# Three wide blocks in place of four, a longer hold for attention matmuls, and a margin in the planner that orders a fused attention and MLP kernel

## The chip, the cores and the metric

One core of a Trainium2 chip runs the whole program. The metric is device time in microseconds, from the start to the end of one execution; a kernel's time is the median of its runs. Engines: PE is TensorE (its weight loads, PEld, overlap its matmuls), DVE is VectorE, ACT is ScalarE, POOL is GpSimd, SP is SyncE, which here issues all DMAs.

## The reference

Linear attention with exponential features (batch B = 8, H = 8 heads, S = 576 tokens, head size D = 64, 128 features and their negatives), then a two-layer MLP on the 4608 tokens with 512 and 2048 columns, all in float32:

```python
def phi(x):
    proj = einsum('bhsd,df->bhsf', x, w_phi)
    proj = proj - max(abs(proj), axis=-1, keepdims=True)
    return concatenate([exp(proj), exp(-proj)], axis=-1)
q_p, k_p = phi(q), phi(k)
kv  = einsum('bhsf,bhsd->bhfd', k_p, v)
z   = sum(k_p, axis=2)
num = einsum('bhsf,bhfd->bhsd', q_p, kv)
den = einsum('bhsf,bhf->bhs', q_p, z)[..., None] + 1e-06
x   = (num / den).transpose(0, 2, 1, 3).reshape(4608, 512)
h   = x @ w_in                       # 512 -> 2048
g   = 0.5 * h * (1 + erf(h / sqrt(2)))
out = g @ w_out                      # 2048 -> 512
```

## The kernel before

**Precision.** An MLP operand is split into a high and a low part in the format fp32r, and a product is three matmuls (high by high, high by low, low by high). Attention matmuls are plain float32 on small shapes, except the later query projections.

**Attention, per batch element** (`attention`). Four heads form a quad (`k_quad`), two a pair (`q_pair`). A quad has five units; each projects keys into the PSUM tile `pk`, DVE takes the maximum (`mx`) and subtracts it (`ek`), ACT makes two exponentials, and small matmuls add into `kv`, which ACT copies to `kvn`. A pair has two halves of 288 tokens: DVE splits the query (`qh`), PE projects it into `pq`, ACT copies it to `pc`, POOL takes a maximum over partitions (`mb`), DVE subtracts, ACT makes exponentials (`ef`), PE multiplies them with `kvn` into `pn`, ACT copies `xo`, and SP writes it to DRAM (`x_d`). The denominators go through DVE and POOL (`un`, `db`) to DRAM, and `quotients` loads them (`dc`), inverts them on DVE and writes `r_d`. From the third batch element on, `pk` and `pq` share one PSUM buffer, the tag `pp`: ten key units and eight query halves use it in turn for each element.

**MLP, narrow** (`block`): 256 tokens, eight units of two of the sixteen column groups. A unit has 24 first-layer matmuls of 256 columns into `ph` (two buffers), two Gelu passes on ACT (`gh`, and `ph` in place), a subtraction on DVE (`gl`), and 12 second-layer matmuls of 512 columns into `po`.

**MLP, wide** (`wide_block`): 512 tokens. The first layer uses seven products in place of eight (Strassen's scheme as Winograd wrote it), on sums of weight blocks that `combos` makes once and stores in DRAM (`s_d`), and on sums of inputs. A unit has 42 first-layer matmuls of 256 columns into `pa` and `pb`, DVE additions that put the outputs together (`u`, `c`), Gelus, and 24 second-layer matmuls into two banks (`po_po`, `po_pp`). Its inputs and the sums `s` lie in buffers that attention used before, so `combos` and the wide blocks are gated on the last 60 operations of attention (`GATE`).

**Order.** Every operation is entered into a planner (`Plan.op`) with an engine, an estimated cost and a rank. `Plan.order` simulates the engines with these costs and picks, at each step, the operation that can start first, and among those that can start within 0.02 us the one with the lowest rank. `emit` then issues everything in that order. On the chip each engine runs its own queue in program order and waits on semaphores; the planner's times are not waited for. PE operations of attention get `PULL` = -2000 on their rank, so they go before MLP matmuls, unless `hold` applies: after an MLP matmul, attention operations wait until those that are ready cost `LUMP` together, or one of them has waited `LINGER`. `plan.since` keeps operations back until a planned time (`WPACE` for each weight, `TF` for the MLP, `HOLD2` for the third and later batch elements). `T0`, `T15`, `LEAD`, `WR`, `ATR`, `WSPAN` set ranks. The ten narrow blocks come first (`2 * JW`), then the four wide ones.

Of the kernel before, what the change touches and what calls it, by code (L numbers as in the profile page):

```python
# [25 lines left out]
DM, DFF = 512, 2048  # L26
# [3 lines left out]
TB = 256  # L30
NBLK = NT // TB
NCC = DM // P
# [27 lines left out]
class Plan:  # L60
# [57 lines left out]
    def order(self, bias):  # L118
# [13 lines left out]
        n = len(self.ops)  # L132
# [40 lines left out]
        while len(done) < n:  # L173
            best = None
            for e, lst in cand.items():
                if not lst:
                    continue
                opts = []
                for o in lst:
                    t = start_of(o)  # L180
                    if t is not None:
                        opts.append((t, o))
                if not opts:
                    continue
                t0 = min(t for t, _ in opts)
                lim = max(t0, clock[e]) + 0.02
                hold = 0.0
                if e == "pe" and last[0] == "f":
                    t_of = {id(o): max(o.ready, first.setdefault(o.n, t)) for t, o in opts}
                    there = [o for t, o in opts if t <= lim and o.kind != "f"]  # L190
                    if sum(o.cost for o in there) < LUMP and all(lim - t_of[id(o)] < LINGER for o in there):
                        hold = 4000.0
                key = None
                for t, o in opts:
                    if t <= lim:
                        k = o.rank
                        if e == "act" and o.table is not None and o.table != table[0]:
                            k += bias
                        if o.kind != "f":
                            k += hold  # L200
                        if key is None or (k, o.n) < key[0]:
                            key = ((k, o.n), t, o)
                if best is None or key[1] < best[1]:
                    best = key
            if best is None:
                raise RuntimeError("no operation can go")
            _, t, o = best
            cand[o.eng].remove(o)
            cost = o.cost
            if o.eng == "act" and o.table is not None and o.table != table[0]:  # L210
                cost += self.SWITCH
                table[0] = o.table
            if o.eng == "pe":
                if self.SHAPE[last[0]] != self.SHAPE[o.kind]:
                    cost += self.BEHIND[last[0]] + self.BEFORE[o.kind]
                last[0] = o.kind
            if o.eng == "dve" and not o.psum:
                for span in taken[-4:]:
                    if t < span[1] - 0.3 and t + cost > span[0] + 0.3 and not span[2]:
                        span[2] = True  # L220
                        cost += BLOCKED
            if o.eng == "pool":
                taken.append([t, t + cost, False])
            o.start, o.end = t, run(t, cost, o.duty) if o.eng == "pe" else t + cost
            if o.nbytes:
                dge[0] = max(dge[0], t) + 0.55
                dma[0] = max(dma[0], dge[0] + 0.75) + o.nbytes / 350.0
                o.late = dma[0] + 0.15 - o.end
            if o.table == "gelu":
                gelus[0] += 1  # L230
                left_at[0] = o.end
            clock[o.eng] = o.end
            for b in o.bufs:
                if b.tag is not None and not b.held:
                    f = slot_free_at[b.tag]
                    b.slot = turn[b.tag]
                    f[b.slot] = None
                    turn[b.tag] = (b.slot + 1) % len(f)
                    b.held = True
                    assert b.line.pop(0) is b  # L240
                b.left -= 1
                if b.left == 0 and b.tag is not None:
                    slot_free_at[b.tag][b.slot] = o.end + o.late + self.HOP[o.eng]
            for u in o.users:
                u.wait -= 1
                u.ready = max(u.ready, o.end + o.late + (self.HOP if u.eng != o.eng else self.SAME)[o.eng])
                if u.wait == 0:
                    cand[u.eng].append(u)
            done.append(o)
# [10 lines left out]
def mm_cost(m, n):  # L260
    return max(0.875 * m, n / 2.306 + 9) / 1e3
# [27 lines left out]
def fused_kernel(ctx: ExitStack, tc: tile.TileContext, qT, kT, va, w_st, w_in, w_out, out):  # L289
# [15 lines left out]
    op = plan.op  # L305
# [60 lines left out]
    wi, wo = {}, {}  # L366
# [223 lines left out]
    NU = NFC // 2  # L590

    def block(j, rank):
# [3 lines left out]
        xh = sb["xh"]([P, NCC, TB], F32R, f"xh_{j}")  # L596
        xl = sb["xl"]([P, NCC, TB], F32R, f"xl_{j}")
        t = j * TB
# [19 lines left out]
        for u in range(NU):  # L618
            rk = rank(u / NU)
            ph = ps["ph"]([P, 2, TB], F32, f"ph_{j}_{u}")  # L620
            for i in range(2):

                def mm1(ph=ph, u=u, i=i):
                    ins = []
                    f = 2 * u + i
                    fs = slice(f % 4 * P, f % 4 * P + P)
                    for c in range(NCC):
                        for w, x in ((0, xh), (0, xl), (1, xh)):
                            ins.append(mm(ph()[:, i, :], lhsT=wi[c, f // 4]()[:, w, fs], rhs=x()[:, c, :], start=len(ins) == 0, stop=len(ins) == 11))
                    return ins  # L630

                op("pe", 12 * mm_cost(128, TB), mm1, r=[xh, xl] + [wi[c, u // 2] for c in range(NCC)], w=[ph], rank=rk)
            gh = sb["gh"]([P, 2, TB], F32R, f"gh_{j}_{u}")
            gl = sb["gl"]([P, 2, TB], F32R, f"gl_{j}_{u}")
            op("act", act(2 * TB, True) + 0.016, lambda gh=gh, ph=ph: nc.scalar.activation(gh(), ph(), AF.Gelu), r=[ph], w=[gh], table="gelu", rank=URGE + rk)  # L635
            op("act", act(2 * TB, True) + 0.037, lambda ph=ph: nc.scalar.activation(ph(), ph(), AF.Gelu), r=[ph], w=[ph], table="gelu", rank=URGE + rk)  # L636
            tt("dve", dve(2 * TB, True), gl, ph, lambda gh=gh: gh().bitcast(F32), ALU.subtract, [ph, gh], [gl], rank=URGE + rk, psum=True)
            for i in range(2):

                def mm2(u=u, i=i, gh=gh, gl=gl):  # L640
                    ins = []
                    f = 2 * u + i
                    for m in range(2):
                        ms = slice(m * P, (m + 1) * P)
                        for g, w in ((gh, 0), (gh, 1), (gl, 0)):
                            ins.append(mm(po()[:, m], lhsT=g()[:, i, ms], rhs=wo[f]()[:, w, :], start=f == 0 and len(ins) % 3 == 0,
                                                        stop=f == NFC - 1 and len(ins) % 3 == 2))
                    return ins

                op("pe", 6 * mm_cost(128, DM), mm2, r=[gh, gl, wo[2 * u + i]], w=[po], rank=rk)  # L650
# [37 lines left out]
    def wide_block(j, rank):  # L688
# [4 lines left out]
        for hh in range(2):  # L693
            x = raw[hh]
# [49 lines left out]
        for u in range(NU):  # L744
# [13 lines left out]
            def product(n, bank, z, first, sides=sides):  # L758
                a, r = sides[n]

                def go():
                    ins = []
                    for i in range(2):
                        for w, x in ((0, 0), (0, 1), (1, 0)):
                            ins.append(mm(bank()[:, z], lhsT=a(i, w), rhs=bs[n]()[:, x, i], start=first and not ins, stop=len(ins) == 5,
                                          skip_group_check=True))
                    return ins

                op("pe", 6 * mm_cost(128, TB), go, r=[*r, bs[n]], w=[bank], rank=rk)

            uu = sb["kvn"]([P, TB], F32, f"u2_{j}_{u}")
            u3 = sb["xo"]([P, TB], F32, f"u3_{j}_{u}")
# [14 lines left out]
            product(4, Bk, 1, False)  # L787
            add(a1, uu, b0, [uu, Bk], [A])
            add(lambda C=C: C()[:, 0], uu, b1, [uu, Bk], [C])
            for f, at, psum in ((f1, A, True), (f2, C, False)):  # L790
                gh = sb["gh"]([P, 2, TB], F32R, f"gh_{j}_{f}")
                gl = sb["gl"]([P, 2, TB], F32R, f"gl_{j}_{f}")
# [3 lines left out]
                for t in range(2):  # L796
# [7 lines left out]
                                              stop=u == NU - 1 and f != f1 and len(ins) % 3 == 2))  # L804
                        return ins

                    op("pe", 6 * mm_cost(128, DM), mm2, r=[gh, gl, wo[f]], w=[po[t]], rank=rk)
        for t in range(2):
            for m in range(2):
                ob = sb["ob"]([P, DM], F32, f"ob_{j}_{t}_{m}")  # L810
# [39 lines left out]


SB = 2
JW = 5
CR = 100.0
CSPAN = 100.0
GATE = 60
T15 = 937.149
BIAS = 40
STICK = 2
PATIENCE = 2.661  # L860
URGE = -1000.0
EARLY = 37.497
WPACE = 2.294
WSPAN = 5.119
WARM = 4
EARLY_PK = ("pp", "po")
EARLY_E = ("ek", "xh", "ek", "xl")
BLOCKED = 0.9
HOLD2 = 26.359
EB = 2  # L870
KB = 0
EPACE = 20.0
TF = 77.984
ND = 2
LUMP = 0.626
LINGER = 0.643
PAIR_K = 0.43
PAIR_Q = 0.7
PAIR_N = 1.18
PAIR_V = 0.125  # L880
PULL = -2000.0
LEAD = 290.175
HOLD = 39.176
WR = -5.223
ATR = -4.775
T0 = 47.571
VERBOSE = False


# [36 lines left out]
```

## Time and profile before

| | before |
|---|---|
| median of 3 runs | 1167.02 us (1164.23 to 1170.59) |
| profiled execution, its own time | 1165.43 us |
| its span, first to last instruction | 1163.7 us |
| mean granted TensorE clock | 0.989 |
| PE busy | 1094.6 us, 94% of the span |
| DVE, ACT, POOL busy | 719.0, 592.9, 327.9 us |

The time lies 1.7 us above the span. A busy PE is not a PE at its peak: matmuls are pipelined, and each record lasts longer than the distance to the next one. The granted clock is the share of full speed that PE was given.

### The profile page before, as it was taken

The numbers are of one execution on the slowest core, as the hardware profiler recorded it, in microseconds if no ns is written. First come the engines' busy times: TensorE is split into PE (matmuls) and PEld (weight loads), VectorE is DVE, ScalarE is ACT, GpSimd is POOL, SyncE is SP. The second block draws the span as 40 slices with busy tenths as digits, with TensorE's granted clock in tenths as the row PEclk, the third lists the DMA queues.
The fourth block names the chain that finished last, engine by engine and source line by source line (L and its number), as shares of the span: only waits on it lengthen the run. The fifth ranks groups of instructions, "written<-read, shape, count | busy, mean of one in ns | idle before, by whom it ended". The sixth has DMA issues, their size and how long they took to land.

```text
span 1163.7 us, 22198 instructions
## 1 busy us (share of the span) xinstructions
PE 1094.6 (94%) x8904; PEld 909.2 (78%) x8904; DVE 719.0 (62%) x1209; ACT 592.9 (51%) x1001; POOL 327.9 (28%) x116
## 2 busy tenths in 40 slices
PE   7888989999999999999989999999999999899997
PEld 4546767877777778877868878889898899798995
DVE  6998999387777676776675644555534534524331
ACT  6876786657676666766757651121222322322322
POOL 2331224166665556765544440000000000000000
PEclk9999999999999999999989999999999999999999
DMA  9974412224233242252131115443724634623420
GB/s 335 338 253 131 111 50 67 82 81 119 68 110 90 79 117 83 64 149 62 53 88 42 53 38 127 145 128 98 209 84 124 184 92 125 185 89 117 128 73 37
DMA packets 117175, 133.98 MB, mean 115 GB/s; under 512 B 28288, under 2 KB 87840, under 8 KB 117072
## 3 DMA queue, kind: packets, MB, share of 16 engines
q1 hardware_dynamic: 117072, 132.56, 38.5%
q8 instruction: 70, 1.15, 0.4%
q14 instruction: 33, 0.27, 0.1%
HBM read 104.96 MB, written 27.56 MB: 114 GB/s over the span
## 4 chain that ended last, share of the span: by engine, by line
PE 59%; DVE 17%; DMA 10%; ACT 4%; issue 4%; SPq 2%; POOL 2%; POOLq 0%; DVEq 0%; ACTq 0%
PE po L308 12%; PE ph L308 9%; PE pb L308 7%; PE po_po L308 7%; PE po_pp L308 7%; PE pa L308 5%; PE kv L308 4%; PE pn L308 3%; DMA qt<-in_qT_dram 3%; PE pq L308 2%; PE pk L308 2%; DVE gl L334 2%; POOL db L548 2%; DVE qh L334 2%; DMA dc<-d_d 1%
## 5 line engine op out<-in xcount | busy, mean ns | idle before, releaser
L308 PE MATMUL ph<-xh,w_i 128*128 128x256 f32 x1280 | 249.0, 285 | 1.8 <-DVE gl L334 1.8
L548 POOL PARTITION_ALL_REDUCE db<-un x48 | 178.4, 3716 | 160.1 <-DVE un L545 120.3
L308 PEld LDWEIGHTS ph<-xh,w_i 128*128 128x128 f32 x1280 | 204.7, 189 | 10.4 <-issue 2.6
L308 PE MATMUL po<-w_o,gh 128*128 128x512 f32 x640 | 207.6, 406 | 2.9 <-ACT ob L328 1.7
L513 POOL PARTITION_ALL_REDUCE mb<-pc x64 | 152.0, 2375 | 205.1 <-ACT pc L328 182.8
L308 PE MATMUL ph<-xl,w_i 128*128 128x256 f32 x640 | 181.4, 283 | 0.0
L308 PE MATMUL po<-w_o,gl 128*128 128x512 f32 x320 | 129.4, 404 | 11.5 <-DVE gl L334 11.5
L308 PEld LDWEIGHTS po<-w_o,gh 128*128 128x128 f32 x640 | 116.4, 192 | 30.1 <-issue 2.4
L793 ACT ACTIVATE gh<-pa 128x512 fp32r<-128x512 f32 x32 | 19.2, 599 | 217.7 <-DVE pa L334 215.3
L308 PEld LDWEIGHTS ph<-xl,w_i 128*128 128x128 f32 x640 | 120.9, 189 | 1.7
L308 PEld LDWEIGHTS kv<-vt,ek 128*64 128x64 f32 (+1 forms) x2560 | 83.5, 137 | 36.6 <-ACT ek L447 17.9
L308 PE MATMUL kv<-vt,ek 128*64 128x65 f32 (+1 forms) x2560 | 94.9, 225 | 10.2 <-ACT ek L447 8.9
L635 ACT ACTIVATE gh<-ph 128x512 fp32r<-128x512 f32 x80 | 47.9, 598 | 108.7 <-PE ph L308 100.6
L308 PE MATMUL pn<-ef,kvn 128*64 128x288 f32 (+1 forms) x512 | 97.0, 422 | 3.3 <-ACT xo L328 1.7
L519 ACT ACTIVATE ef<-pc 128x576 f32<-128x576 f32 x128 | 81.7, 679 | 33.6 <-DVE pc L334 33.3
L334 DVE TENSOR_TENSOR pa<-u,pb 128x256 f32<-128x256 f32 x32 | 13.7, 428 | 130.8 <-PE pb L308 130.8
L447 ACT ACTIVATE ek<-ek 128x512 f32<-128x512 f32 (+1 forms) x120 | 69.4, 586 | 47.1 <-DVE ek L334 45.6
L334 DVE TENSOR_TENSOR gl<-ph,gh 128x512 fp32r<-128x512 f32 x80 | 54.9, 687 | 50.0 <-ACT ph L636 47.2
L308 PEld LDWEIGHTS po<-w_o,gl 128*128 128x128 f32 x320 | 61.1, 191 | 31.2 <-DVE gl L334 17.5
L430 DVE TENSOR_REDUCE mx<-pk 128x4 f32<-128x512 f32 (+1 forms) x80 | 50.5, 631 | 53.5 <-PE pk L308 53.3
L308 PE MATMUL po_po<-w_o,gh 128*128 128x512 f32 x256 | 80.0, 394 | 1.1 <-ACT gh L793 1.1
L308 PE MATMUL pb<-b,s 128*128 128x256 f32 x576 | 79.1, 282 | 2.0 <-DMA s<-s_d 1.9
(90 smaller groups left out, 1905.2 us busy)
## 6 DMA issues: line engine op xcount, KB each, us to landing
s<-s_d SPq DMA_DIRECT2D x128, 256.0 KB
qt<-in_qT_dram SPq DMA_DIRECT2D x112, 144.0 KB
vt<-in_va_dram SPq DMA_DIRECT2D x16, 585.0 KB
kt<-in_kT_dram SPq DMA_DIRECT2D x16, 576.0 KB
out_dram<-ob SPq DMA_DIRECT2D x36, 256.0 KB
raw_i<-in_w_in_dram SPq DMA_DIRECT2D x16, 512.0 KB
raw_o<-in_w_out_dram SPq DMA_DIRECT2D x16, 512.0 KB
x_d<-xo SPq DMA_DIRECT2D x48, 144.0 KB
```

What stands on the lines that cost most here:

```text
L308: return tc.keep_in_program_order(nc.tensor.matmul(*a, **kw))
L334: op(eng, cost, lambda: e.tensor_tensor(out=dst(), in0=a(), in1=b(), op=o), r=r, w=w, **kw)
L430: op("dve", dve(256 * n, True), lambda xs=xs, mx=mx: nc.vector.tensor_reduce(out=mx()[:, 0].rearrange("p (j i) -> p j i", j=2), in_=xs(), ...
L447: op("act", act(256 * n, b < SB), lambda at=at, es=es, s=s: nc.scalar.activation(es[s](), at(), AF.Exp, scale=1.0 - 2.0 * s), r=[of], w=[e ...
L513: op("pool", 2.2, lambda mb=mb, pc=pc: nc.gpsimd.partition_all_reduce(mb(), pc(), P, bass_isa.ReduceOp.absmax), r=[pc], w=[mb], **k(1))
L519: op("act", act(2 * HS), lambda ef=ef, pc=pc, s=s: nc.scalar.activation(ef()[:, s], pc(), AF.Exp, scale=1.0 - 2.0 * s), r=[pc], w=[ef], ta ...
L548: op("pool", 3.7, lambda db=db, un=un: nc.gpsimd.partition_all_reduce(db(), un(), P, bass_isa.ReduceOp.add), r=[un], w=[db], **k())
L635: op("act", act(2 * TB, True) + 0.016, lambda gh=gh, ph=ph: nc.scalar.activation(gh(), ph(), AF.Gelu), r=[ph], w=[gh], table="gelu", rank= ...
L793: op("act", act(2 * TB, psum) + 0.016, lambda gh=gh, at=at: nc.scalar.activation(gh(), at(), AF.Gelu), r=[at], w=[gh], table="gelu", rank= ...
```

## The change

`JW` goes from 5 to 6: twelve narrow blocks and three wide ones in place of ten and four. `LUMP` and `LINGER` go from 0.626 and 0.643 us to 2.5 and 3.0 us. In the planner, an operation of PE that uses the result of another engine counts as ready 0.8 us later (`MARGIN`), from planned time 130 on; a buffer that comes free is not delayed so. First-layer matmuls get the rank of a point 1.5 units earlier (`AHEAD`, `AHEADW`). In the last unit of a wide block the second layer is entered by output bank first, in the others by column group first as before. The constants of rank and pace are replaced.

```diff
-                u.ready = max(u.ready, o.end + o.late + (self.HOP if u.eng != o.eng else self.SAME)[o.eng])
+                u.ready = max(u.ready, o.end + o.late + (self.HOP if u.eng != o.eng else self.SAME)[o.eng] + (MARGIN if u.eng == "pe" != o.eng and o.end > 130.0 else 0.0))
...
-                op("pe", 12 * mm_cost(128, TB), mm1, r=[xh, xl] + [wi[c, u // 2] for c in range(NCC)], w=[ph], rank=rk)
+                op("pe", 12 * mm_cost(128, TB), mm1, r=[xh, xl] + [wi[c, u // 2] for c in range(NCC)], w=[ph], rank=rank((u - AHEAD) / NU))
...
-                op("pe", 6 * mm_cost(128, TB), go, r=[*r, bs[n]], w=[bank], rank=rk)
+                op("pe", 6 * mm_cost(128, TB), go, r=[*r, bs[n]], w=[bank], rank=rank((u - AHEADW) / NU))
...
+            second = []
...
-                    op("pe", 6 * mm_cost(128, DM), mm2, r=[gh, gl, wo[f]], w=[po[t]], rank=rk)
+                    second.append((t, f != f1, mm2, [gh, gl, wo[f]]))
+            for t, _, go, r in sorted(second, key=lambda x: x[:2] if u == NU - 1 else (x[1], x[0])):
+                op("pe", 6 * mm_cost(128, DM), go, r=r, w=[po[t]], rank=rk)
...
-JW = 5
+JW = 6
+AHEAD = 1.5
+AHEADW = 1.5
+MARGIN = 0.8
...
-T15 = 937.149
+T15 = 901.4
...
-PATIENCE = 2.661
+PATIENCE = 2.5
...
-EARLY = 37.497
-WPACE = 2.294
-WSPAN = 5.119
+EARLY = 37.5
+WPACE = 3.996
+WSPAN = 24.5
...
-HOLD2 = 26.359
+HOLD2 = 0.0
...
-TF = 77.984
+TF = 90.0
...
-LUMP = 0.626
-LINGER = 0.643
+LUMP = 2.5
+LINGER = 3.0
...
-LEAD = 290.175
-HOLD = 39.176
-WR = -5.223
-ATR = -4.775
-T0 = 47.571
+LEAD = 167.4
+HOLD = 44.6
+WR = -13.5
+ATR = -21.1
+T0 = 57.4
```

## Rows read from the trace of the kernel before

**Rows 1.** Busy time by stretch (stretch, length, PE PEld DVE ACT POOL, PEclk, DMA, GB/s)
```profile
90.00:180.00 90.00, 79.73 (x677) 62.01 (x678) 84.27 (x140) 70.75 (x120) 21.59 (x8) 0.96 0.33 88
180.00:693.00 513.00, 490.07 (x4556) 399.59 (x4555) 354.21 (x530) 342.19 (x518) 278.32 (x93) 0.99 0.29 82
693.00:808.00 115.00, 110.21 (x703) 98.48 (x702) 62.37 (x121) 24.20 (x45) 0.28 (x1) 1.00 0.43 120
808.00:1164.00 356.00, 341.05 (x2111) 303.46 (x2110) 142.88 (x296) 91.15 (x178) 0.00 (x0) 1.00 0.41 120
```

**Rows 2.** Chain that ended last, 780 to 860 us (start, us, what)
```profile
792.33 5.71 PE ph L308 x48
798.04 5.54 PE po L308 x24
```

**Rows 3.** PE busy time by stretch, matmuls of tile ph alone
```profile
90.00:693.00 603.00, 193.35 (x1463) 0.98 0.29 83
693.00:808.00 115.00, 55.66 (x460) 1.00 0.43 120
```

**Rows 4.** The same for kv, pk, pn and pq, in this order
```profile
90.00:693.00 603.00, 72.18 (x1984) 0.98 0.29 83
...
90.00:693.00 603.00, 40.75 (x432) 0.98 0.29 83
...
90.00:693.00 603.00, 69.73 (x424) 0.98 0.29 83
...
90.00:693.00 603.00, 40.72 (x208) 0.98 0.29 83
```

**Rows 5.** What PE waited for, 90 to 693 us (total, times, longest)
```profile
PE pq L308 <- DVE ek L334: 9.7, 8, 4.3
PE po L308 <- DVE gl L334: 8.4, 7, 2.2
```

**Rows 6.** What PE waited for, 693 to 1164 us
```profile
PE po_po L308 <- DVE gl L334: 5.0, 7, 1.5
PE po L308 <- DVE gl L334: 3.1, 4, 1.3
```

**Rows 7.** Timeline of PE, end of the span
```profile
1157.54 0.40 PE L308 MATMUL po_pp<-w_o,gl 128*128 128x512 f32 x1
```

**Rows 8.** Timeline of ACT, end of the span
```profile
1156.58 1.07 ACT L328 COPY ob<-po_po 128x512 f32<-128x512 f32 x2 [3.58 <-PE po_po L308]
1159.29 1.21 ACT L328 COPY ob<-po_pp 128x512 f32<-128x512 f32 x2 [1.63 <-DMA out_dram<-ob]
```

**Rows 9.** Timeline of PE, 240 to 280 us (start, us)
```profile
240.79 1.19 PE L308 MATMUL pn<-ef,kvn 128*64 128x288 f32 x8
241.91 0.71 PE L308 MATMUL pk<-wst,kt 64*128 64x128 f32 x8
...
248.74 0.28 PE L308 MATMUL ph<-xh,w_i 128*128 128x256 f32 x1
248.94 1.19 PE L308 MATMUL pn<-ef,kvn 128*64 128x288 f32 x8
...
250.29 0.28 PE L308 MATMUL ph<-xl,w_i 128*128 128x256 f32 x1
```

**Rows 10.** Granted clock in a short stretch (stretch, length, PE busy, PEclk, DMA, GB/s)
```profile
605.00:609.00 4.00, 4.00 (x12) 0.55 0.02 2
```

**Rows 11.** Timelines of PE, DVE and POOL, around 528 and 600 us
```profile
603.50 1.30 PE L308 MATMUL pq<-qh,wd 128*128 128x288 f32 x4 [4.33 <-DVE ek L334]
...
528.80 2.64 DVE L334 TENSOR_TENSOR qh<-qt,qh 64x576 fp32r<-64x576 f32 x1
...
597.18 1.03 DVE L568 TENSOR_SCALAR dc<-dc 128x18 f32<-128x18 f32 x1 [3.93 <-DMA dc<-d_d]
...
528.03 3.85 POOL L548 PARTITION_ALL_REDUCE db<-un  x1
```

**Rows 12.** Instructions on tile qh, DVE (count: min/median/max ns, first and last start)
```profile
L334 DVE TENSOR_TENSOR qh<-qt,qh x48: 754/756/2968, 133.4 to 670.7; 64x576 fp32r<-64x576 f32 x48
```

## Prediction

> **What bounds the kernel now.** I read the busy time by stretch first. From 693 us on only MLP work is left (POOL, which serves attention, has 0.28 us there), and PE is busy for 110.2 of 115 us and then 341.05 of 356 [rows 1]. Before that, from 90 to 693 us, attention and narrow blocks share PE: 79.73 + 490.07 = 569.8 us busy of 603, 33.2 idle [rows 1]. PE is the engine that sets the end; DVE is close behind only from 90 to 180 (84.27 of 90), while the weights are split, and falls to 354.21 of 513 after that [rows 1].
>
> Busy time hides how fast PE really goes, so the second view is the chain that ended last: 48 first-layer matmuls pass in 5.71 us, 0.119 us each, and 24 second-layer ones in 5.54 us, 0.231 each [rows 2]. A narrow block has 192 and 96 of them: 22.8 + 22.2 = 45.0 us. In 90 to 693, 1463 first-layer matmuls ran [rows 3], 7.6 blocks, hence 343 us; attention's own PE time is 72.18 + 40.75 + 69.73 + 40.72 = 223.4 us [rows 4]. With the idle 33.2 that is 600 of the 603 us, so the account closes. What can be won without less work is that idle, the holes inside attention's visits, and about 5 us on either side of 808 us.
>
> The third view is who PE waits for. Nearly all of it comes from DVE: query projections for the shared bank that DVE has yet to read (9.7 us in 8 waits, the longest 4.3) and second-layer matmuls for `gl` (8.4 in 7) [rows 5], and after 693 again `gl`, 5.0 + 3.1 in 11 [rows 6]. The queue of PE is written out by the planner, so an operation placed before its input is there stops everything behind it, first-layer matmuls included that were ready.
>
> **The change part by part.** The sum goes against the profiled execution's own 1165.4 us; the median of the runs shown is 1.6 us above it, and I add that at the end.
>
> *One wide block becomes two narrow ones.* A wide block has 8 units of 42 first-layer matmuls, 336; two narrow ones have 384. The second layer is the same, 192. So PE gets 48 x 0.119 = **+5.7 us** of work at full rate, and nothing hides it, since PE sets the end. The planner only orders; it can't take that back.
>
> *Block boundaries.* In 693 to 808, 460 first-layer matmuls ran [rows 3], 2.4 narrow blocks with 4.8 us idle: 2.0 each. In 808 to 1164 the idle is 15.0 us [rows 1], of which 6 lie behind the last matmul near 1158 [rows 7]: 9 over four wide blocks, 2.2 each. Swapping one for two gives 4.0 - 2.2 = **+1.8**.
>
> *The last unit of a wide block by bank.* `po_po` is now complete two groups of six second-layer matmuls (2 x 1.39) before the end in place of one. At the end of the span ACT copies `po_po` at 1156.58, then waits for the output DMA to free the two `ob` buffers, and copies `po_pp` at 1159.29 [rows 8], though its last matmul ended at 1157.9 [rows 7]. With `po_po` copied 1.4 us earlier, this wait of 1.63 us nearly goes: **-1.3**. In exchange the second column group's Gelus have only one group of six matmuls to hide behind; if they don't, the next late thing is `gl` of that group, at most 1.4 us back. Bounds: 0 to -1.6.
>
> *Margin and first layer ahead.* Second-layer matmuls are now placed as if `gl` came 0.8 us later, and first-layer matmuls of the next unit go ahead of them. The chip doesn't wait for planned times, so the margin costs nothing by itself; the work that fills is 12 first-layer matmuls, 1.43 us, already waiting with a free `ph`. The waits concerned add up to 8.4 + 5.0 + 3.1 = 16.5 us in 18, 0.9 each [rows 5, 6]. Below: all vanish, 16.5. Above: nothing, if DVE is late by more than the order allows. I take half, **-8**, since the longest waits (2.2, 1.5, 1.3) exceed the margin. If the cover is gone (no free `ph`), the first layer itself waits for `gl`, and nothing is won.
>
> *Holding attention.* An attention operation that comes after an MLP matmul is now held until 2.5 us of company are ready or 3.0 us have passed. This covers what the margin doesn't: the bank that comes free. Of the 9.7 us of `pq` waits the longest is 4.3 [rows 5]; a hold of up to 3.0 leaves little of the others. Below: the 9.7 and a part of the 15 us of small waits that the two rows don't list (33.2 - 18.1), say 17; above: nothing. I take **-8**. Behind a held projection stand DVE's `mx` and `ek`, ACT's exponentials and `kv`; they are late by the same, which matters only if attention runs out of time (a rival below).
>
> *Visits to PE.* Between first-layer matmuls a `pn` group takes from 248.74 + 0.12 to 250.29 - 0.12, 1.31 us; followed by `pk` it takes 1.12 (240.79 to 241.91) [rows 9]. So a visit costs about 0.19 us beyond its work. The shared bank is used 18 times per batch element, 108 times for six, so I estimate some 110 visits now. Of 223.4 us in portions of at least 2.5 there are at most 89: 20 fewer; at 54, half, it would be 10 us. I take 20 x 0.19 = **-4**, bounds 0 and -10. The Trainium skill (TensorEngine Tiling (Array Packing), Key Properties) says that a change of tiling mode drains TensorE, which would hold between `pn` and `pk` as well. By that, merging two visits saves one change of four and not half of the price, so -2 and a sum 2 us higher; the rows show no more for `pn` before `pk` than 1.12 us.
>
> *Clock.* After long waits the granted clock falls to the lower of its two levels, 1.2 GHz, for a while: 0.55 of full speed on average in 605 to 609 [rows 10], behind the wait of 4.33 us that ended at 603.50 [rows 11]. By the stretches, 0.04 x 90 + 0.01 x 513 = 8.7 us of PE's rate are lost [rows 1]. With the longest waits shortened I take **-3**, bounds 0 and -8.7.
>
> *Slower weights, MLP from planned 90 in place of 78.* DVE splits the weights at 84.27 of 90 us busy [rows 1], so later loads hide behind DVE, and attention gets DVE's time instead: I take 0. If the cover fails, the MLP starts 12 us later (the difference of `TF`), of which attention fills a part. Bounds: -5 (earlier loads of queries) to +12.
>
> Sum: 1165.4 + 5.7 + 1.8 - 1.3 - 8 - 8 - 4 - 3 = 1148.6, and with 1.6 for the median **1150 us**, 1.4% less than before.
>
> **The rivals.**
>
> *The order moves the waits but doesn't remove them.* DVE is late by more than any margin here: the subtraction of `qh` takes 0.756 us as a rule and up to 2.968 [rows 12]; at 528.80 it took 2.64 beside POOL's all-reduce of 3.85 us [rows 11]. And DVE stands in its own queue: 3.93 us for the denominators' DMA until 597.18, just ahead of PE's wait of 4.33 [rows 11]. A margin of 0.8 doesn't hold 1.9 or 3.9. Then margin, hold and clock give nothing: 1165.4 + 5.7 + 1.8 - 1.3 - 4 = 1167.6, 1169 for the median. Against it: most waits are short (0.9 on average), and the hold is longer. The Trainium skill (SBUF — State Buffer, Terms, the shared port pair) calls this an exclusive lock, in which the later of the two engines is blocked for the whole instruction. By that rule a DVE operation can be late by all of an all-reduce, which points to this rival; the 2.64 us agree.
>
> *Attention comes too late.* Today 108 uses of the shared bank take 603 us, 5.6 each. The hold grows by up to 2.4 us (3.0 - 0.643). Twelve narrow blocks, attention and today's idle give 540 + 223 + 33 = 796 us of PE; so attention outlasts them once a use takes 796 / 108 = 7.4 us, 1.8 more than now. At 2.4 more, narrow work ends near 862 (573 us of it and 0.258 of the time for attention), with 11 uses left; unheld, they take 62 us, in which PE has 24 us of work, and the wide blocks still need their sums, gated on attention: some 20 us of DVE (62.37 busy in 693 to 808 [rows 1], a third of it). About 58 us idle: near 1208, slower. Against it: during a visit nothing is held, so one visit can serve two uses, and the planner falls back to attention where PE has nothing else.
>
> *The start loses its cover.* The 12 us of `TF` appear and half of the gains fails: 1150 + 12 + 11 = 1173.
>
> **Chances and range.** The forecast's mechanism 0.57 (own range 1130 to 1161); waits only moved 0.19 (1163 to 1172); start 0.12 (1161 to 1180); attention late 0.12 (1180 to 1225). A measurement of this kernel can tell about 0.5%, 1161.2 to 1172.9, from no change. Faster: 0.57. Same: 0.15 of the second, 0.05 of the third, 0.20 together. Slower: 0.04 + 0.07 + 0.12 = 0.23. All bounds below at once give 1165.4 + 7.5 - 1.6 - 16.5 - 17 - 10 - 8.7 - 5 + 1.6 = 1116; I set the low end at 1124 and the high end at 1186, where the early part of the late case begins.
>
> **What would show it.** First-layer matmuls 2304 in narrow tiles and 1008 in wide ones; `po` waits for `gl` below 8 us in the mixed stretch; `pq` waits for DVE below 4; fewer, longer visits; no stretch with a clock near 0.6; attention over before the twelfth narrow block. Wrong would be: PE idle between the last `pn` and the first `pa`, a first `ph` 12 us later than before, or the waits back under other names.

## The result, and the profile after

The median fell from 1165.62 us (4 runs, 1161.07 to 1170.59) to 1148.99 us (4 runs, 1147.43 to 1151.56): a ratio of 0.9867, 95% interval 0.9837 to 0.9898. The forecast was 1150. The profiled execution spans 1145.7 us, 18.0 less than before.

The page of the changed kernel: engine, busy time, share and instructions; the granted clock in 40 slices.

```profile
PE 1097.1 (96%) x8952; PEld 920.4 (80%) x8952; DVE 696.2 (61%) x1153; ACT 662.2 (58%) x1045; POOL 321.5 (28%) x116
...
PEclk9998987999999999999999999999999999999999
```

PE has 48 more matmuls than before and is busy 2.5 us longer, in a span 18.0 us shorter. The clock digits below 9 all lie in the first seven slices, the first 200 us.

Busy time of PE by stretch, first of the kernel before and then of the changed one (stretch, length, busy, granted clock, DMA share, GB/s):

```profile
90.00:210.00 120.00, 107.72 (x964) 0.97 0.34 92
210.00:693.00 483.00, 462.08 (x4271) 0.99 0.28 81
```

```profile
90.00:210.00 120.00, 103.91 (x858) 0.89 0.45 131
210.00:693.00 483.00, 481.75 (x4426) 1.00 0.30 84
```

Most of the result stands in these lines. From 210 to 693 us the idle falls from 20.9 to 1.25 us and the clock stays full. From 90 to 210 us the changed kernel is worse: 16.1 us idle in place of 12.3, at a clock of 0.89. The stretches [rows 1] gave 33.2 us idle from 90 us to attention's end; now attention ends at 771 us, and PE is busy for 76.97 + 586.68 = 663.65 us of the 681 before that, 17.35 idle:

```profile
90.00:180.00 90.00, 76.97 (x663) 59.02 (x662) 74.88 (x123) 61.88 (x108) 18.44 (x8) 0.90 0.54 160
180.00:771.00 591.00, 586.68 (x5263) 492.56 (x5262) 378.14 (x572) 442.50 (x625) 276.37 (x94) 0.99 0.27 77
```

What PE waited for in the changed kernel (total, times, longest), the largest from 90 to 210 us and then all from 210 to 771 us:

```profile
PE pq L308 <- DVE ek L334: 10.4, 3, 4.8
PE pq L308 <- DMA qt<-in_qT_dram: 3.8, 1, 3.8
...
PE pk L308 <- DVE ek L334: 1.1, 2, 0.6
```

Against [rows 5], the waits of `po` for `gl` are gone from the mixed stretch (90 us to attention's end), and those of `pq` for the shared bank, 9.7 us in 8, have become three long ones, 10.4 us, all before 210 us. At such waits the clock falls, as the granted clock around them shows:

```profile
153.00:157.00 4.00, 2.33 (x7) 0.56 0.73 211
174.00:178.00 4.00, 2.21 (x10) 0.50 0.00 0
194.00:198.00 4.00, 2.44 (x10) 0.56 0.21 61
```

0.50 is 1.2 GHz, the lower level. How far the start falls behind is seen in the matmuls done by 210 us, tiles `ph`, `po` and `kv`, the kernel before first, then the changed one:

```profile
0.00:210.00 210.00, 38.50 (x276) 0.98 0.58 183
0.00:210.00 210.00, 30.19 (x114) 0.98 0.58 183
0.00:210.00 210.00, 36.91 (x960) 0.98 0.58 183
```

```profile
0.00:210.00 210.00, 37.41 (x264) 0.90 0.56 173
0.00:210.00 210.00, 26.66 (x94) 0.90 0.56 173
0.00:210.00 210.00, 34.15 (x832) 0.90 0.56 173
```

12 first-layer, 20 second-layer and 128 `kv` matmuls fewer: 1.4 + 4.6 us of MLP work at the rates of [rows 2], and 128 of the 2560 matmuls of `kv`.

Behind 693 us the idle falls too, from 19.4 to 12.3 us of each span. The waits for `gl` there, 8.1 us before [rows 6], are 0.6 us in the changed kernel, from 771 us on:

```profile
PE po L308 <- DVE gl L334: 0.6, 1, 0.6
```

So the change lost time at the start (6.4 us more idle by 210 us) and won more than that behind it (19.7 us less up to 693, 7.2 after).

### The profile page after: what moved, and what is told of

Read it like the earlier page. It is cut to its first block, busy times and chain, and to the rows that moved or that the text cites. A ratio compares the mean times of both kernels' runs of the same rounds, so it can differ in the third digit from the quotient of the medians.

```text
span 1145.7 us, 22254 instructions
## 1 busy us (share of the span) xinstructions
PE 1097.1 (96%) x8952; PEld 920.4 (80%) x8952; DVE 696.2 (61%) x1153; ACT 662.2 (58%) x1045; POOL 321.5 (28%) x116
## 4 chain that ended last, share of the span: by engine, by line
PE 72%; DVE 9%; DMA 6%; issue 4%; SPq 3%; ACT 3%; POOL 2%; DVEq 0%; ACTq 0%; POOLq 0%
PE po L308 18%; PE ph L308 18%; PE kv L308 6%; PE pb L308 5%; PE po_pp L308 5%; PE pn L308 5%; PE po_po L308 5%; PE pa L308 4%; PE pq L308 3%; PE pk L308 3%; POOL mb L513 1%; SPq L708 1%; DMA qt<-in_qT_dram 1%; DMA rp<-r_d 1%; DVE gl L334 1%
## 5 line engine op out<-in xcount | busy, mean ns | idle before, releaser
L308 PE MATMUL ph<-xh,w_i 128*128 128x256 f32 x1536 | 299.9, 284 | 1.6 <-DVE gl L334 1.2
L308 PEld LDWEIGHTS ph<-xh,w_i 128*128 128x128 f32 x1536 | 248.2, 190 | 9.6 <-issue 2.2
L308 PE MATMUL po<-w_o,gh 128*128 128x512 f32 x768 | 246.4, 402 | 1.9 <-ACT ob L328 1.9
L308 PE MATMUL ph<-xl,w_i 128*128 128x256 f32 x768 | 218.7, 285 | 0.0
L308 PEld LDWEIGHTS po<-w_o,gh 128*128 128x128 f32 x768 | 137.7, 190 | 31.4 <-issue 2.2
L308 PE MATMUL po<-w_o,gl 128*128 128x512 f32 x384 | 152.9, 398 | 0.6 <-DVE gl L334 0.6
L308 PEld LDWEIGHTS ph<-xl,w_i 128*128 128x128 f32 x768 | 146.1, 190 | 3.3
L308 PEld LDWEIGHTS kv<-vt,ek 128*64 128x64 f32 (+1 forms) x2560 | 85.6, 140 | 36.7 <-ACT ek L447 14.1
L308 PEld LDWEIGHTS po<-w_o,gl 128*128 128x128 f32 x384 | 73.0, 190 | 18.5 <-DVE gl L334 1.6
L794 ACT ACTIVATE gh<-pa 128x512 fp32r<-128x512 f32 x24 | 14.4, 599 | 123.1 <-PE po_pp L308 86.1
L334 DVE TENSOR_TENSOR pc<-pc,mb 128x576 f32<-128x576 f32 x64 | 65.4, 1021 | 29.7 <-POOL mb L513 29.4
L308 PEld LDWEIGHTS pn<-ef,kvn 128*64 128x64 f32 (+1 forms) x512 | 39.6, 139 | 32.5 <-issue 7.5
```

The lines of the kernel that those rows point to most:

```text
L308: return tc.keep_in_program_order(nc.tensor.matmul(*a, **kw))
L334: op(eng, cost, lambda: e.tensor_tensor(out=dst(), in0=a(), in1=b(), op=o), r=r, w=w, **kw)
L794: op("act", act(2 * TB, psum) + 0.016, lambda gh=gh, at=at: nc.scalar.activation(gh(), at(), AF.Gelu), r=[at], w=[gh], table="gelu", rank= ...
```

## The experiments

All compare with the kernel before on the same chip. To set them side by side I multiply ratios by 1162 us, near the median of the kernel before in these runs (1161.5 to 1162.4); the changed kernel is then at 1146.5.

| kernel | ratio to before | interval | us |
|---|---|---|---|
| changed | 0.9867 | 0.9837 to 0.9898 | 1146.5 |
| changed, T15 nudged | 0.9893 | 0.9859 to 0.9928 | 1149.6 |
| changed, no margin | 0.9959 | 0.9942 to 0.9976 | 1157.2 |
| changed, short hold | 1.0139 | 1.0111 to 1.0166 | 1178.2 |
| changed, no first layer ahead | 1.0022 | 0.9998 to 1.0046 | 1164.6 |
| changed, four wide blocks | 1.0240 | 1.0206 to 1.0274 | 1189.9 |
| changed, start of before | 0.9810 | 0.9786 to 0.9834 | 1139.9 |
| changed, paced by rank | 1.0595 | 1.0560 to 1.0630 | 1231.1 |
| changed, paced by rank, earlier | 1.0062 | 1.0047 to 1.0077 | 1169.2 |
| before, margin alone | 1.0266 | 1.0225 to 1.0307 | 1192.9 |
| before, three wide blocks | 1.0027 | 1.0011 to 1.0042 | 1165.1 |
| before, three wide blocks and long hold | 0.9934 | 0.9919 to 0.9948 | 1154.3 |
| changed, start of before, free buffers at the end | 0.9785 | 0.9768 to 0.9802 | 1137.0 |

**How much is chance of an order?**

```diff
-T15 = 901.4
+T15 = 899.0
```

> The changed kernel with T15 at 899.0 in place of 901.4, a change of pace of 0.3% that means nothing: PE's order differs in places. It tells how much of any difference here is the chance of an order. If orders hardly matter: within 2 us of the changed kernel. Rival: the planner is so sensitive that any nudge moves the time by 5 us or more; then differences of that size mean nothing in the other runs.

1149.6, 3 us above the changed kernel, with intervals that overlap. A difference of 3 us or less is not read as a cause below. One nudge is one sample: how far other orders would move the time is not known.

**The margin taken away.**

```diff
-MARGIN = 0.8
+MARGIN = 0.0
```

> The changed kernel with MARGIN = 0. If the planner's margin is what emptied the mixed stretch, its waits come back: PE idle in 210 to 770 us from under 2 us to 10 to 20, second-layer matmuls waiting for gl at their head, and the time 6 to 12 us above the changed kernel's 1149. Rival: the hold and the first layer ahead already give the room, so the time stays within 3 us. Rival: DVE's lateness comes from the constants of rank, then no difference either.

10.7 us slower, within the first theory's range, but not by the waits that it named. What PE waited for in this kernel from 210 to 771 us:

```profile
PE pq L308 <- DVE ek L334: 5.2, 2, 3.5
PE pk L308 <- DVE ek L334: 1.2, 1, 1.2
```

No wait of `po` for `gl` is back. What came back are attention's own waits. So with the first layer ahead, the margin does not show as protection of the second layer, and attention waits more without it; why, no run shows. Two cautions: the traced execution is the longest of this kernel's twelve, 5 us above their median, and PE is also idle 4.4 us longer before 210 us.

**The first layer ahead taken away.**

```diff
-AHEAD = 1.5
-AHEADW = 1.5
+AHEAD = 0.0
+AHEADW = 0.0
```

> The changed kernel with AHEAD and AHEADW at 0, so first-layer matmuls rank with their own unit. If they are the filler behind the margin, second-layer matmuls stand closer to gl and 2 to 5 us of waits come back, 1151 to 1154. Rival: with two buffers of ph the first layer goes ahead anyway as soon as it may, so nothing changes, 1149 within 2.

18 us slower: both expectations were far too small. From 210 to 771 us `po` waits for `gl` only 0.7 us, but `ph` now waits for it:

```profile
PE ph L308 <- DVE gl L334: 4.1, 4, 1.8
```

Most of the loss lies in the wide blocks. First and last start of the first product's tile and of the second bank, the changed kernel and then this one:

```profile
L308 PE MATMUL pa<-b,w_i x288: 274/279/393, 877.2 to 1128.5; 128*128 128x256 f32 x144
...
L308 PE MATMUL po_pp<-w_o,gl x96: 387/392/403, 895.2 to 1139.5; 128*128 128x512 f32 x96
```

```profile
L308 PE MATMUL pa<-b,w_i x288: 274/280/360, 886.3 to 1146.7; 128*128 128x256 f32 x144
...
L308 PE MATMUL po_pp<-w_o,gl x96: 387/392/404, 901.8 to 1162.7; 128*128 128x512 f32 x96
```

The three wide blocks take 262.3 us with the first layer ahead and 276.4 without, 14.1 of the 21.8 us by which the traced executions differ (the one without is the longest of its twelve). From start to start in the timeline, the 1008 `pa` and `pb` matmuls fill 119.4 us with it and 138.8 without. My reading is that with the margin in the planner products of the same unit look late, and without a rank that lets the next unit's products fill, the order has holes; no run shows this reading by itself. The kernel before, with neither, had its wide blocks fairly full (15.0 us idle in 356, tail included [rows 1]).

**The hold taken away.**

```diff
-LUMP = 2.5
-LINGER = 3.0
+LUMP = 0.626
+LINGER = 0.643
```

> The changed kernel with LUMP and LINGER back at 0.626 and 0.643 us. If the hold keeps PE from standing at the shared bank, pq and pk wait for DVE again for some 8 us between 210 and 770 us and visits go from 109 to about 115: 8 to 12 us slower, 1157 to 1161. Rival: the visits are set by the shared bank and hardly change (114 before, 109 after), and the hold only delays attention: within 4 us, or faster if attention's delay cost something.

32 us slower, three times what I expected. What PE waited for from 210 us to attention's end at 671:

```profile
PE pq L308 <- DVE ek L334: 11.4, 12, 3.9
PE pk L308 <- DVE ek L334: 5.8, 7, 2.0
```

The waits are those that the theory named, 17.2 us against 1.1 with the hold. The traced executions differ by 24.4 us, less than the medians: 20.4 us of idle, 19.6 of it from 210 to 693 us, and 4.0 of busy time. Beyond that the traces don't show where the 32 us go.

**Three wide blocks alone, and with the hold.** The kernel before, first with

```diff
-JW = 5
+JW = 6
```

and then with the long hold besides.

> The kernel before with JW at 6 and nothing else. There attention ends near 690 us and the cover of narrow blocks is not needed, so the term of the prediction should show alone: 5.7 us of work and 1.8 of boundaries, a ratio of 1.005 to 1.008. Rival: twelve narrow blocks share the time with attention better, and it is no slower.

> The kernel before with JW at 6 and the long hold, without margin, without the first layer ahead and with the old constants. If the hold is worth what its removal cost (31 us with margin and first layer ahead in place), this is 10 to 25 us faster than the same without the hold. Rival: hold, margin and first layer ahead pay only together, as the margin alone did not pay (a ratio of 1.027 on the kernel before): then it is no faster than before, or slower.

Three wide blocks alone cost 0.0027 of 1162, 3.1 us (1.3 to 4.9), less than the 7.5 of the prediction and no more than the nudge moved the time. The hold on top gains 10.8 us. From 210 to 733 us these two wait as follows, the one without the hold first:

```profile
PE pq L308 <- DVE ek L334: 8.1, 7, 4.1
PE po L308 <- DVE gl L334: 6.2, 5, 2.0
```

```profile
PE po L308 <- DVE gl L334: 6.9, 8, 2.9
PE pq L308 <- DVE ek L334: 2.9, 2, 2.5
```

This separates the two: the hold takes the shared bank's waits from 8.1 to 2.9 us and leaves those for `gl` as they were. The runs above point to the first layer ahead for these: without the margin none is back, and without the first layer ahead they stand at `ph`. The hold gains 10.8 us here and 32 in the changed kernel; the two pairs differ in margin, first layer ahead, start and the other constants, so no run shows which of these makes the difference.

**The margin alone, on the kernel before.**

```diff
 JW = 5
+MARGIN = 0.8
```

> The kernel before with the margin of 0.8 us alone: four wide blocks, short hold, no first layer ahead, old constants, old order in the last unit. If the margin takes waits for gl away by itself, 4 to 8 us faster than before. Rival: without the first layer ahead there is no filler in the pure MLP stretch and without the hold the shared bank still stops PE, so within 4 us of before or slower.

2.7% slower, worse than the rival. As in the run without the first layer ahead, the waits for `gl` move to `ph`, where they were 1.8 us before (from 90 to 693 us; here from 100 to 1160):

```profile
PE ph L308 <- DVE gl L334: 8.6, 5, 2.8
```

Those of `po` are 2.8 us, and the shared bank's `pq` waits rise to 18.6 us in 16. So a margin without filler makes worse orders, in both runs that have it.

**Four wide blocks in the changed kernel.**

```diff
-JW = 6
+JW = 5
```

> The changed kernel with JW back at 5, four wide blocks. By the work, PE has 48 first-layer matmuls less (5.7 us) and one boundary of 2.2 us in place of two of 2.0: 7 to 8 us faster, about 0.6%. Rival: a wide block's boundary costs more once the rest has no waits (the changed kernel still waits 1.5 to 2.4 us at each), and attention needs the cover of narrow blocks: no faster, or up to 5 us slower.

43 us slower, where the work said 7 less and the rival at most 5 more. Attention ends at 771 us as in the changed kernel, but narrow blocks end at 788 in place of 886. PE in the hole, and its waits from 780 to 890 us:

```profile
790.00:890.00 100.00, 60.13 (x330) 0.78 0.56 160
```

```profile
PE pa L308 <- DMA s<-s_d: 27.7, 2, 15.0
PE pa L308 <- DVE gl L334: 8.4, 3, 5.3
PE pa L308 <- DVE b L330: 5.5, 1, 5.5
```

39.9 us of 100 are idle, at a clock of 0.78. This is the prediction's rival "attention comes too late", in the kernel that has the hold without the two further narrow blocks: the sums are gated on attention, and nothing covers them.

**Attention paced by rank, without company.** Short hold, `PULL` at 0; then with attention's rank earlier.

```diff
-PULL = -2000.0
+PULL = 0.0
...
-LEAD = 167.4
+LEAD = 290.175
```

> The changed kernel with the short hold, and PULL at 0 in place of -2000, so attention's matmuls compete with the MLP's by rank and are paced without being gathered. With the short hold alone it was about 31 us slower than the changed kernel, and attention ended at 671 in place of 771 us. If the hold's gain is the slower pace of attention, which leaves DVE and ACT more room, half or more of the 31 us comes back: 1148 to 1162 on this scale. Rival: the company is what counts (fewer switches, room at the shared bank), then it stays above 1165.

> As the kernel paced by rank (short hold, PULL at 0), with LEAD at 290.175 in place of 167.4, so attention ranks some 120 us earlier. That kernel had almost no idle PE while attention ran, but attention ended at 893 us, behind the narrow blocks, and PE then stood for 63 us. If pace is what counts, an end some 100 us earlier takes those 63 us away with the mixed stretch still full: a ratio to the kernel before of 0.985 to 1.00. Rival: company is what counts, the mixed stretch fills with waits as soon as attention goes faster, and the ratio stays above 1.01, near the short hold's 1.014.

The first is 5.9% slower, and shows both things at once:

```profile
210.00:880.00 670.00, 668.09 (x5698) 1.00 0.23 67
880.00:1000.00 120.00, 50.01 (x256) 0.67 0.44 125
```

While attention runs, PE has 1.9 us idle in 670: a slow pace alone empties the mixed stretch of idle, without any gathering; attention makes 148 visits to PE there, and 109 in the changed kernel. Then attention ends at 893 us, behind the narrow blocks, and PE is idle for 70 of 120 us. With the earlier rank that hole is gone and the ratio is 1.0062, just above the range that the pace theory gave and below the rival's. From 300 to 820 us PE is busy for 515.00 of 520 us; more idle lies before:

```profile
0.00:300.00 300.00, 256.14 (x2544) 0.93 0.50 153
300.00:820.00 520.00, 515.00 (x4344) 1.00 0.23 68
```

The changed kernel has 264.89 us busy by 300, so about 9 of the 18 us by which the traced executions differ lie there. So pace counts, and what company adds beyond it is not separated by these runs.

**The start of before in the changed kernel.**

```diff
-EARLY = 37.5
-WPACE = 3.996
-WSPAN = 24.5
+EARLY = 37.497
+WPACE = 2.294
+WSPAN = 5.119
...
-HOLD2 = 0.0
+HOLD2 = 26.359
...
-TF = 90.0
+TF = 77.984
...
-WR = -13.5
-ATR = -21.1
-T0 = 57.4
+WR = -5.223
+ATR = -4.775
+T0 = 47.571
```

> The changed kernel with the constants of the start as before: WPACE, WSPAN, WR, ATR, T0, TF, HOLD2, EARLY. At 210 us the changed kernel is some 14 us of PE work behind the one before, with clock stretches at half after three waits at the shared bank between 154 and 194. If the slower weights cause that, the first 210 us give back 8 to 14 us: 1135 to 1141. Rival: the long hold is the cause, as attention is held while no MLP work is ready; then the three waits stay and the time is within 4 us of 1149. Rival: T0 also moves the pace of attention against the blocks, and what the start gives back is lost later.

6.6 us faster than the changed kernel, less than the 8 to 14 expected, and faster than both kernels. By 210 us it has done 288 `ph`, 121 `po` and 896 `kv` matmuls:

```profile
0.00:210.00 210.00, 37.62 (x288) 0.95 0.55 179
0.00:210.00 210.00, 34.77 (x121) 0.95 0.55 179
0.00:210.00 210.00, 34.87 (x896) 0.95 0.55 179
```

That is more MLP work than in either of the two kernels, and the first `ph` starts at 102.8 us, as before (103.0) and not at 112.1. The price: 483 - 475.44 = 7.6 us idle from 210 to 693 us in place of 1.25. It is the third theory in part: some of the start's gain is lost later. And the start is not free of waits either; the shared bank stops PE there under another name (from 90 to 210 us):

```profile
PE pk L308 <- ACT pc L328: 7.9, 2, 6.2
```

The edit restores eight constants together; which of them gives the 6.6 us is not separated.

**Free buffers at the end.** On top of that, the last block's second bank goes into buffers that nothing uses any more.

```diff
-                ob = sb["ob"]([P, DM], F32, f"ob_{j}_{t}_{m}")
+                ob = sb[("xr", "rb")[m] if t == 1 and j == NBLK // 2 - 1 else "ob"]([P, DM], F32, f"ob_{j}_{t}_{m}")
```

> The changed kernel with the start of before (0.981 in its run), and the last block's second bank copied into two buffers that are free by then (tags xr and rb) in place of ob. In the changed kernel ACT still waits 1.69 us at the end for the output DMA to free ob, so the order by bank did nothing there. If that wait is all that stands there, the span behind the last matmul shrinks by 1.7 us and the ratio is 0.978 to 0.981. Rival: the output DMAs themselves end last, and nothing is won.

0.9785, the fastest of all. The last copy on ACT, in the changed kernel, in the kernel with the start of before, and in this one:

```profile
1141.28 1.15 ACT L328 COPY ob<-po_pp 128x512 f32<-128x512 f32 x2 [1.69 <-DMA out_dram<-ob]
```

```profile
1133.18 1.20 ACT L328 COPY ob<-po_pp 128x512 f32<-128x512 f32 x2 [1.64 <-DMA out_dram<-ob]
```

```profile
1130.81 1.07 ACT L328 COPY ob<-po_pp 128x512 f32<-128x512 f32 x2 [0.33 <-PE po_pp L308]
```

The wait for the DMA to free `ob` is gone, and the copy starts 0.33 us after the one before it and no longer 1.64. Against the kernel without the free buffers the time is 2.9 us less, with intervals that overlap; the rows show 1.3 us of it.

## Why the prediction was right

The time came out 1 us from the forecast, and part of that is luck. The terms, on the scale of the table, with what the runs measured on one way from the kernel before to the changed one (three wide blocks, hold, then the rest, the start last):

| term | forecast | measured |
|---|---|---|
| third wide block gone: work and boundaries | +7.5 | +3.1 alone |
| hold, visits | -8, -4 | -10.8 on the old constants |
| margin, first layer ahead, clock (with the new pace and the last unit's order) | -8, -3 | 1154.3 to 1139.9: -14.4 |
| last unit by bank | -1.3 | 0 by the rows |
| slower weights and later MLP | 0, bounds -5 to +12 | +6.6, for the eight constants of the start together |
| sum | -16.8 | -15.5 |

*Luck.* The lines miss by -4.4, +1.2, -3.4, +1.3 and +6.6 us, which add up to +1.3. On another way they differ: taken out of the changed kernel, the hold is worth 31.7 us and the margin 10.7.

*Right in mechanism.* PE's idle in the mixed stretch was what could be won, and from 210 us on the two waits of [rows 5] went. The hold acts on those at the shared bank: with it alone they fall from 8.1 to 2.9 us, and without it 17.2 us come back. Those for `gl` went with margin and first layer ahead together; by the runs that take out one of the two, the first layer ahead removes them, and the margin alone moves them to `ph`, as the prediction said of a lost cover. The account of PE at full rate held: from 210 to 693 us, with 1.25 us idle, the clock is 1.00.

*Signs.* There are 2304 first-layer matmuls in narrow tiles and 1008 in wide ones, `po` hardly waits for `gl`, and attention is over before the twelfth narrow block. Two signs failed, both at the start: `pq` waited 10.4 us for DVE, not below 4, and there are stretches at 0.50 and 0.56. The first `ph` came 9 us later, near the 12 that were named as a sign of being wrong.

*Mis-sized.* The term for margin and first layer ahead was too small. I took half of the waits for `gl` on the ground that the longest exceed the margin; of the 16.5 us of [rows 5, 6], 0.6 is left at `po` and 1.2 at `ph`. The prediction also said that nearly all that PE waits for comes from DVE; by its own trace the waits for DVE from 90 to 693 us add up to 22.6 of 33.2 us idle.

*The rival on DVE's lateness.* It did not come about, though DVE is no more punctual: from 90 us to attention's end 18 subtractions of `qh` and `pc` take over 1.2 us in the timeline, against 17 before, and PE waits 1.1 us in the 561 from 210 to 771. The exclusive lock of the Trainium skill (SBUF — State Buffer, Terms, the shared port pair) fits the longer subtractions; the time to which it pointed, 1169, did not follow from them. All 35 ran beside an all-reduce of POOL. They ended 0.2 to 0.5 us before its record did, the 2.64 us of [rows 11] among them, so blocking to the very end of the all-reduce is not what these rows show; spans on POOL are rough.

*Wrong step: visits to PE.* Counted in the timeline, attention's visits between MLP matmuls go from 114 to 109, not to 89. A held operation goes after 3.0 us even without company, so portions of 2.5 us were no bound. With the hold alone on the old constants the count is 96, near the forecast; in the changed kernel only 5 visits serve both a key and a query projection, against 18 there. No run isolates what a visit costs. The rule of the Trainium skill on draining (TensorEngine Tiling (Array Packing), Key Properties) thus could not be weighed by this change; no run here shows it.

*Wrong step: the last unit.* The term forgot that the new order of entry only breaks ties. The planner takes what can start first, and the second bank's matmuls of the first column group are ready before the first bank's of the second. The banks alternate to the end as before, and ACT's wait is 1.69 us, as it was 1.63 [rows 8]. What removes it is a free buffer.

*Wrong step: the start at 0, and with it the clock.* I let DVE's full load hide the slower weights. It doesn't: the first `ph` came 9 us later, and the bank's three waits with a halved clock behind them lie there. The hold alone does not make these waits: with the short hold 7.0 us of them remain before 210 us, and with the hold on the old constants there are none. So the clock, forecast at -3, went the other way: granted over the whole run it fell from 0.989 to 0.980, and from 0.98 to 0.90 in the first 210 us; with the start of before it is 0.988. The bounds of the start covered it, the value did not.

*The rival that mattered.* "Attention comes too late" did not happen in the changed kernel: attention ended at 771 us, with 432 of 2304 first-layer matmuls left, 101 us of narrow work at 45.0 a block. It happens as soon as that cover is gone: with four wide blocks, and with attention paced by rank. So at this pace of attention the two further narrow blocks are the hold's condition and not only a cost. The rival counted this cover, but the terms priced the blocks and the hold one by one.

*Open.* Whether three wide blocks alone cost less than the 5.7 us of work because some wait of before went with them, or by the chance of an order; the runs don't tell. Why taking out the hold costs 32 us in the changed kernel and 10.8 on the old constants: the waits account for 16 of the 24.4 us that the traces show. And whether the hold on the old constants, where attention ends at 733 us, needs the two further narrow blocks: four wide blocks with the hold were run at the new pace alone.

## What to carry to other kernels

Where an order is written out ahead and the bound engine waits for others now and then, it pays to place its work later than the estimates say, but only with other work ranked to fill the room: the margin alone made this kernel 2.7% slower, and beside the filler and the hold it was worth 10.7 us. Slowing the side work so that it spreads under the bound engine's work was worth more here than finishing it early, as long as what it gates was still covered; that cover has to be counted in the same account. A bundle of changes should be undone part by part: here one part, the constants of the start, cost 6.6 us that the others paid for.

## What the runs showed of the hardware

The granted clock can fall to half after waits shorter than I had thought. The third of the three waits was 1.88 us long:

```profile
194.38 1.21 PE L308 MATMUL pq<-qh,wd 128*128 128x288 f32 x4 [1.88 <-DVE ek L334]
```

The clock was 1.00 from 190 to 194 us and 0.56 from 194 to 198. The length of a wait does not decide alone: in the kernel before, one of 2.24 us that ended at 434.71 was followed by 0.59 in the next 4 us, and one of 2.24 us that ended at 524.07 by 1.00.

ACT took 69 us more (662.2 in place of 592.9), and nearly all of it is the loading of function tables: 152 loads of 1.283 us in place of 100, 66.7 us. The largest group, before and then changed:

```profile
L635 ACT ACT_TABLE_LOAD x50 | 64.2, 1283 | 5.1 <-PE ph L308 4.3
```

```profile
L635 ACT ACT_TABLE_LOAD x76 | 97.5, 1283 | 1.5 <-PE ph L308 0.3
```

With the hold alone on the old constants there are 100 as well, and 108 in the changed kernel without the first layer ahead. From 210 to 693 us, where PE is idle for 1.25 us, they cost no time.
